# Sums for the last two batches of a fused attention and ELU-MLP kernel: taken off GpSimd, spread over three places

## The chip, the cores and the metric

The kernel runs on one core of a Trainium2 chip. The metric is the device time of one execution in microseconds (us). TensorE multiplies, VectorE (DVE in the rows) and ScalarE (ACT) work on tiles, GpSimd (POOL) can do the same as VectorE but reads no PSUM, and SyncE (SP) issues the transfers.

## The reference

Attention over 8 batches, 12 heads, 448 positions and 64 features, then an MLP over all 3584 tokens:

```python
q_n, k_n = rmsnorm(q, g_q), rmsnorm(k, g_k)
scores = q_n @ k_n.T / sqrt(64)
attn = exp(scores - max); attn = attn / (sum + 1e-9)
x = (attn @ v)                    # reshaped to (3584, 768)
h = x @ w_in                      # 768 -> 2048
g = where(h > 0, h, exp(min(h, 0)) - 1)
out = g @ w_out                   # 2048 -> 768
```

All inputs and outputs are float32.

## The kernel before

Every float32 operand of a large matmul is held as two float16 tiles, a high half and a low half (`whi`/`wli` for W_in, `who`/`wlo` for W_out, the two planes of a `gts` tile for g), and each product is three matmuls: high times high, high times low, low times high. One batch is 448 columns wide, so a matmul has a 128x128 weight tile and 448 moving columns.

The work is software-pipelined by hand. A table `SCHED` gives a half-step number to each small operation of a tile, and at each half step the kernel issues what is due and a few matmuls of the MLP of an earlier batch. Within one engine the instructions run in the order in which they were issued. Attention (scores, softmax, transposes by DMA, product with v) of a batch overlaps the MLP of the batch before it, with TensorE as the common resource.

The last two batches, 6 and 7, share their second layer (`mlp_two`). W_out is cut into quarters, and g of both batches into halves; seven block products replace eight (Strassen's scheme in Winograd's form). This needs sums of W_out's quarters (`t1` to `t4`, for each of three row groups d = 0, 1, 2) and sums of the g tiles of both batches (named `t1`, `t2` and `c22` in `sums`, beside the ones that overwrite `gts`).

- The sums of W_out's quarters are made in pieces while attention still runs (`piece_sums`, `SCHED["sums"]`). VectorE adds high and low halves, GpSimd scales and adds, ScalarE and GpSimd split the result into halves again, and SyncE stores them to DRAM (`kept`).
- During the first layer of batch 7 (`first_layer` with `m1_last`) they are loaded into the rooms of W_in that have been used up (`t_load`).
- In that same first layer each of the 16 results goes through ScalarE (exp), VectorE (the ELU), and then all the sums of g: GpSimd adds the halves of batch 6's g (`full`), forms more sums and some low halves; ScalarE forms high halves; VectorE forms the rest. `last1` and `last2` list at which half step behind the matmul each of these is issued.
- Then come 15 products of 24 matmuls each, TensorE alone; VectorE combines their banks into output tiles (`more`, line 907), and SyncE stores them (`store`).

TensorE's line 1015 is the first layer of batches 6 and 7; line 1027 is `product`. A PSUM bank is used by product after product, and a product waits until VectorE has read the bank's former content.

Of the kernel before, what the change touches and what calls it, by code (L numbers as in the profile page):

```python
# [33 lines left out]
def tile_attention_then_elu_mlp(ctx: ExitStack, tc: tile.TileContext, qk, v, v_scan, gg, w_in, w_out, out):  # L34
# [100 lines left out]
    staging = rooms[NE + 1].bitcast(F16)[:, :512].rearrange("p (i n) -> p i n", i=2)  # L135
# [665 lines left out]
    def joint_scales():  # L801
# [14 lines left out]
    kept = [  # L816
        {q: dram.tile([128, 2, KF * 128], F16, name=f"{q}{d}") for q in ("t1", "t2", "t3", "t4")}
        for d in range(3)
    ]
    tail = raws[:, 5 * S : 5 * S + 768].bitcast(F32)  # L820

    def piece_sums(d, k):

        A, Y, Z = (tail[:, a : a + 256] for a in range(0, 768, 256))

        def full(o, row, kh):
            rows = slice(kh * KF + 2 * k, kh * KF + 2 * k + 2)
            h, l = (t[d + 3 * row][:, rows].rearrange("p f n -> p (f n)") for t in (who, wlo))
            nc.vector.tensor_tensor(out=o, in0=h, in1=l, op=ALU.add)
# [9 lines left out]
        def split(o, q):  # L839
            return [  # L840
                lambda: nc.scalar.activation(staging[:, 0], o, AF.Copy),
                lambda: tt(staging[:, 1], o, staging[:, 0], ALU.subtract),
                lambda: nc.sync.dma_start(
                    out=kept[d][q][:, :, 256 * k : 256 * k + 256], in_=staging
                ),
            ]
# [18 lines left out]
        (0, "t3"), (0, "t4"), (1, "t3"), (1, "t4"), (0, "t1"), (0, "t2"),  # L865
        (1, "t1"), (1, "t2"), (2, "t3"), (2, "t4"), (2, "t1"), (2, "t2"),
    ]
    part = {dq: units[i] for i, dq in enumerate(T_ORDER)}
    h_now, t_left = [0], []

    def t_load(d, q):
        for i in (0, 1):
            nc.sync.dma_start(
                out=part[d, q][i].rearrange("p c n -> p (c n)"), in_=kept[d][q][:, i]
            )
# [52 lines left out]
    sums, temps, spots = {}, [], []  # L928

    def spaces():  # L930
        def flat(n, tag, shape, dt, k, bufs):
            t = pool.tile(shape, dt, tag=tag, name=n, bufs=bufs)
            names = " ".join(f"d{i}" for i in range(len(shape) - 1))
            t = t.rearrange(f"p {names} -> p ({names})")
            if dt == F16:
                t = t.bitcast(F32)
            return [t[:, i * S : i * S + S] for i in range(k)]

        nat_shape = [128, 2, NJ, D]
        qkt_shape = [128, 3, NJ, 128]  # L940
        spots.extend(rooms)
        spots.extend(ptall[:, i * S : i * S + S] for i in range(7))
        spots.extend(flat("sq", "qkt", qkt_shape, F16, 3, 2))
        t = [as_f32(places.pop(0)) for _ in range(3)]
        t += flat("rn", "nat", nat_shape, F32, 2, 2) + flat("rm", "nat", nat_shape, F32, 2, 2)
        t += flat("rt", "t16", [128, 2, NJ, 2, D], F16, 2, 1)
        t += flat("rq", "qkt", qkt_shape, F16, 3, 2)
        temps.append(t[:6])
        temps.append(t[6:])

    def m1_last(k, f, ph):
        sc, ui2 = (t[:, a : a + 1] for t, a in ((mscale[B - 1][0], f), (mscale[B - 1][1], 0)))
        if not spots:
            spaces()
        c = f % KF
        low = f < KF
        g = gts[f]
        e1, e2, r1, r2, r3, r4 = temps[c % 2]
        e = e1 if low else e2
        three = [as_f16(spots[i]) for i in range(3 * c, 3 * c + 3)]  # L960
        sums.update(zip([("t1", c), ("t2", c), ("c22", c)], three))
# [9 lines left out]
        def third():  # L971
            nc.vector.scalar_tensor_tensor(
                out=e, in0=ph[:, :S], scalar=sc, in1=e, op0=ALU.mult, op1=ALU.max
            )

        def full(o):
            nc.gpsimd.tensor_tensor(out=o, in0=g[:, 0], in1=g[:, 1], op=ALU.add)

        def stt(o, x, s1, y, op):
            nc.vector.scalar_tensor_tensor(out=o, in0=x, scalar=s1, in1=y, op0=ALU.mult, op1=op)  # L980

        def high(o, x, s1=1.0):
            nc.scalar.activation(o[:, 0], x, AF.Copy, scale=s1)

        def low_of(eng, o, x):
            eng.tensor_tensor(out=o[:, 1], in0=x, in1=o[:, 0], op=ALU.subtract)
# [7 lines left out]
        o1, o2, o3 = three  # L994
        return "last2", 0, [
            one, two, third, lambda: full(r4),
            lambda: high(g, e, ui2),
            lambda: nc.gpsimd.tensor_tensor(out=r3, in0=e1, in1=e2, op=ALU.add),
            lambda: stt(g[:, 1], e, ui2, g[:, 0], ALU.subtract),
            lambda: high(o1, r3, ui2), lambda: stt(r1, r3, ui2, r1, ALU.subtract),  # L1000
            lambda: high(o2, r1),
            lambda: nc.gpsimd.tensor_tensor(out=r4, in0=r4, in1=r1, op=ALU.subtract),
            lambda: stt(o1[:, 1], r3, ui2, o1[:, 0], ALU.subtract),
            lambda: high(o3, r4), lambda: low_of(nc.vector, o2, r1),
            lambda: low_of(nc.gpsimd, o3, r4),
        ]

    def first_layer(b, order, result):
        for k, f in enumerate(order):
# [11 lines left out]
            while t_left and t_left[0][0] <= k:  # L1021
                t_load(*t_left.pop(0)[1])
# [10 lines left out]
    def mlp_two():  # L1033
# [9 lines left out]
        t_left.extend((-(-4 * (i + 1) // 3) - 1, dq) for i, dq in enumerate(T_ORDER))  # L1043
# [3 lines left out]
        for h in range(h_now[0] + 1, h_now[0] + 12):  # L1047
            now, tasks[h] = tasks.get(h, []), []
            for fn, args in now:
                fn(*args)  # L1050
        banks = sb[:4] + [av] + mb
# [11 lines left out]
        for d, q in (  # L1063
            (0, "t3"), (0, "t4"), (1, "t3"), (1, "t4"), (0, "t1"), (0, "t2"), (0, "c22"),
            (1, "t1"), (1, "t2"), (1, "c22"), (2, "t3"), (2, "t4"), (2, "t1"), (2, "t2"),
            (2, "c22"),
        ):
            bank = made[d, q] = banks[n % 8]
            n += 1
            for _ in product(bank, lambda c: w_of(d, q, c), lambda c: b_of(q, c)):  # L1070
                yield None
            ub, uj = uas[d][1:]
            if q == "t2":
                u2, u3, u4 = (as_f32(places.pop(0)) for _ in range(3)) if d < 2 else ys[0]
                ys[d] = u2, u3, u4
                more(u2, bank, c11[d], uj)
                more(u4, made[d, "t1"], u2, uj)
                more(u3, made[d, "t3"], u2, uj)
                for k, row in (("t4", d), ("t1", d + 3)):
                    y = pool.tile([128, S], F32, tag="e", name="y", bufs=3)  # L1080
                    more(y, made[d, k], u3, uj)
                    store(y, row, B - 1)
# [115 lines left out]

    a, n = SCHED["sums"]
# [496 lines left out]
```

## Time and profile before

| | us |
|---|---|
| median of 3 runs (1229.64 to 1232.92) | 1229.67 |
| the profiled execution's own time | 1229.63 |
| its span, first to last instruction | 1227.8 |
| TensorE busy | 1168.1 |
| VectorE busy | 1024.3 |
| ScalarE busy | 815.0 |
| GpSimd busy | 729.0 |

Busy times are sums over the whole span. The stages differ: attention and MLP overlap until about 1088 us, the first layer of batch 7 has TensorE from there to about 1149 us, and the 15 products stand from there to the end.

### The profile page before, as it was taken

To read this page: it belongs to the slowest core of one execution; us is meant where nothing else is said; L and a number is where in the kernel's file an instruction comes from. 1 tells how busy PE (TensorE), PEld (TensorE's weight loads), DVE (VectorE), ACT (ScalarE), POOL (GpSimd) and SP (SyncE) were. 2 spreads that over 40 slices of the span, in tenths; PEclk is the share of its full clock that TensorE was granted. 3 is DMA by queue.
4 is the path that set the end of the run, shared out by engine and by line. 5 is a ranking of instruction groups with operands and counts; after the bars stand their busy time and mean duration, and the time that the engine had idled before them with its cause. 6 is when DMAs were issued, how large, how long until landed. Compare 5 with 4: busy or idle time off the path is not lost. (4 is left out here: it accounts for less than half of the span.)

```text
span 1227.8 us, 22061 instructions
## 1 busy us (share of the span) xinstructions
PE 1168.1 (95%) x7108; PEld 608.5 (50%) x7108; DVE 1024.3 (83%) x2122; ACT 815.0 (66%) x1792; POOL 729.0 (59%) x985
## 2 busy tenths in 40 slices
PE   3789999999999999999999999999999999998898
PEld 2556555555555554554444554445445545554454
DVE  7999998989986699879997899878998789649812
ACT  6999999757775577657675677666775677624400
POOL 5887668645453366756666666766566663328800
PEclk9999999999999999999999999999999999999999
DMA  7886788877777877897669876897769976533101
GB/s 252 254 240 185 188 177 200 192 162 170 141 161 176 170 149 148 176 209 158 133 154 208 185 153 130 185 205 155 142 152 190 192 146 129 103 86 103 52 23 45
DMA packets 422260, 195.85 MB, mean 160 GB/s; under 512 B 370048, under 2 KB 401536, under 8 KB 422144
## 3 DMA queue, kind: packets, MB, share of 16 engines
q1 hardware_dynamic: 422144, 194.45, 70.8%
q8 instruction: 56, 0.92, 0.3%
q14 instruction: 60, 0.49, 0.1%
HBM read 74.65 MB, written 17.30 MB: 75 GB/s over the span
## 5 line engine op out<-in xcount | busy, mean ns | idle before, releaser
L630 POOL TENSOR_SCALAR st<-st 128x1 f32<-128x1 f32 x294 | 82.7, 281 | 263.6 <-ACT w32s L626 217.9
L626 ACT ACTIVATE w32s<-s,st 128x448 f32<-128x448 f32 x242 | 152.1, 629 | 121.9 <-DVE st L610 103.9
L610 DVE TENSOR_REDUCE st<-s 128x1 f32<-128x448 f32 x336 | 203.5, 613 | 30.9 <-PE s L603 22.2
L1116 PE MATMUL m<-gall,whos 128*128 128x448 f16 x768 | 209.7, 353 | 0.0
L676 DVE SCALAR_TENSOR_TENSOR raws<-w32s,st,raws 128x448 f16<-128x448 f32 x199 | 179.5, 903 | 29.3 <-ACT raws L670 28.3
L1103 PEld LDWEIGHTS <-whis 128*128 128x128 f16 x1152 | 111.2, 98 | 110.8 <-issue 11.4
L1116 PEld LDWEIGHTS <-whos 128*128 128x128 f16 x1152 | 111.0, 98 | 107.9 <-issue 8.3
L1103 PE MATMUL m<-x,whis 128*128 128x448 f16 x578 | 157.6, 353 | 2.4 <-DVE e L759 2.4
L670 ACT ACTIVATE raws<-w32s,st 128x448 f16<-128x448 f32 x199 | 130.7, 660 | 22.0 <-DVE st L638 5.1
L1116 PE MATMUL m<-gall,wlos 128*128 128x448 f16 x384 | 135.4, 353 | 0.0
L603 PE MATMUL s<-qkt 128*64 128x448 f16 (+1 forms) x496 | 108.9, 363 | 12.4 <-DMA qkt<-t 4.9
L408 POOL TENSOR_TENSOR nat<-nat,r 128x896 f32<-128x896 f32 (+1 forms) x48 | 88.5, 1844 | 31.1 <-DVE r L398 23.9
L1116 PE MATMUL s<-gall,whos 128*128 128x448 f16 x384 | 105.3, 353 | 0.4 <-DVE gall L770 0.4
L1103 PE MATMUL m<-x,wlis 128*128 128x448 f16 x289 | 101.9, 353 | 0.0
L703 PE MATMUL av<-ptall,vt 128*64 128x448 f16 x924 | 96.2, 353 | 1.4 <-issue 1.2
L764 ACT ACTIVATE gall<-e,ui 128x448 f16<-128x448 f32 x96 | 63.5, 663 | 36.9 <-DVE e L759 36.6
L1103 PEld LDWEIGHTS <-wlis 128*128 128x128 f16 x576 | 56.3, 98 | 54.2 <-issue 3.3
L1116 PEld LDWEIGHTS <-wlos 128*128 128x128 f16 x576 | 56.3, 98 | 54.1 <-issue 3.2
L770 DVE SCALAR_TENSOR_TENSOR gall<-e,ui,gall 128x448 f16<-128x448 f32 x96 | 78.5, 819 | 1.2 <-ACT gall L764 1.2
L1103 PE MATMUL s<-x,whis 128*128 128x448 f16 x286 | 77.8, 352 | 0.3 <-DVE e L759 0.2
L703 PEld LDWEIGHTS <-vt 128*64 128x64 f16 x924 | 54.0, 110 | 37.3 <-issue 5.6
L1116 PE MATMUL s<-gall,wlos 128*128 128x448 f16 x192 | 67.7, 353 | 0.0
(330 smaller groups left out, 2758.7 us busy)
## 6 DMA issues: line engine op xcount, KB each, us to landing
nat<-in_qk SPq DMA_DIRECT2D x48, 448.0 KB, 4.5
raws<-in_w_out SPq DMA_DIRECT2D x24, 512.0 KB, 4.3
qkt<-qkt SPq DMA_DIRECT2D x96, 112.0 KB, 4.0
out<-y SPq DMA_DIRECT2D x48, 224.0 KB, 2.4
vn<-in_v SPq DMA_DIRECT2D x38, 256.0 KB, 2.9
vscan<-in_v_scan SPq DMA_DIRECT2D x36, 224.0 KB, 3.2
whos<-in_w_in SPq DMA_DIRECT2D x10, 768.0 KB, 7.5
t<-wts SPq DMA_DIRECT2D x48, 128.0 KB, 2.3
```

Of the source, the lines that this page charges most:

```text
L408: nc.gpsimd.tensor_tensor(out=n[:, a:], in0=n[:, a:], in1=r[:, a:], op=ALU.mult)
L603: nc.tensor.matmul(ps[r0 : r0 + n, :S], lhs, qq[:, 1, h * S : h * S + S], start=(t == 0), stop=(t == 2),)
L610: nc.vector.tensor_reduce(out=st[:, 0:1], in_=pss[T][:, :S], axis=AX.X, op=ALU.max, negate=True)
L626: nc.scalar.activation(e, ps, AF.Exp, bias=st[:, 0:1], accum_out=st[:, 1:2])
L630: (nc.vector if by_pe(T) else nc.gpsimd).tensor_scalar(out=st[:, 1:2], in0=st[:, 1:2], scalar1=1e-9, scalar2=2.0 ** (UP - 7) if by_pe(T) e ...
L670: nc.scalar.activation(p16[:, :S], e, AF.Copy, scale=stats[T][:, 2:3])
L676: nc.vector.scalar_tensor_tensor(out=p16[:, S:], in0=e, scalar=r, in1=p16[:, :S], op0=ALU.mult, op1=ALU.subtract)
L703: nc.tensor.matmul(av[64 * h : 64 * h + 64, :S], vs[:, h], ps[h], start=(k == 0), stop=(k == len(terms) - 1),)
L764: nc.scalar.activation(g[:, 0], e, AF.Copy, scale=1.0 if b == 0 else ui)
L770: nc.vector.scalar_tensor_tensor(out=g[:, 1], in0=e, scalar=ui, in1=g[:, 0], op0=ALU.mult, op1=ALU.subtract)
L1103: nc.tensor.matmul(ph[:, :S], w[:, c, :], x[:, r, :], start=(c == 0 and i == 0), stop=last)
L1116: nc.tensor.matmul(py[:, :S], w, g[:, r, :], start=(f == 0 and i == 0), stop=last)
```

## The change

W_out's sums: a piece is now 32 columns of all eight row blocks, so that its scale is one column of `rho`; VectorE does the additions and two fused multiply-adds, ScalarE the two remaining multiplications, GpSimd nothing. The sums are stored to DRAM in float32 and not split; splitting into halves follows after the load (`t_half`: a load, a ScalarE copy, a VectorE subtraction, in three staging tiles). Each of the 24 loads brings half of one quarter's sum: 12 are issued during batch 7's first layer, 12 behind it, in groups of three.

Sums of g: the additions of batch 6's halves (`full`, 16 of them) move to VectorE and ahead of batch 7's first layer. In the layer itself only the ELU, the two sums that overwrite `gts` and r3 stay. The sums `t2`, `t1` and `c22` are formed after the layer (`late_sums`). GpSimd has nothing to do in this tail.

The products change order: `t3` and `t4` of all three d come first, then `t2`, `t1`, `c22` for each d; banks are given by a list.

```diff
-    staging = rooms[NE + 1].bitcast(F16)[:, :512].rearrange("p (i n) -> p i n", i=2)
...
         def tt(o, x, y, op):
-            nc.gpsimd.tensor_tensor(out=o, in0=x, in1=y, op=op)
+            nc.vector.tensor_tensor(out=o, in0=x, in1=y, op=op)
+
+        def stt(o, x, i, y, op):
+            nc.vector.scalar_tensor_tensor(
+                out=o, in0=x, scalar=rho(i), in1=y, op0=ALU.mult, op1=op
+            )
 
         def mul(o, i):
-            o = o.rearrange("p (f r n) -> p f r n", f=2, r=4)
-            r = scales[f"rho{i}"][:, 4 * d : 4 * d + 4]
-            tt(o, o, r.unsqueeze(1).unsqueeze(3).broadcast_to([128, 2, 4, 32]), ALU.mult)
...
+            nc.scalar.activation(o, o, AF.Copy, scale=rho(i))
...
-            lambda: mul(A, 1), lambda: tt(Z, Z, Y, ALU.subtract), lambda: mul(Y, 2),
-            lambda: tt(Y, Y, A, ALU.subtract), lambda: mul(Z, 2),
-            *split(Y, "t1"),
-            lambda: tt(A, Z, A, ALU.add), lambda: full(Y, 0, 1),
-            *split(Z, "t3"),
-            lambda: mul(Y, 1), lambda: tt(Y, Y, A, ALU.subtract),
-            *split(A, "t2"), lambda: None, lambda: None,
-            *split(Y, "t4"),
+            lambda: mul(A, 1), lambda: tt(Z, Z, Y, ALU.subtract),
+            lambda: stt(Y, Y, 2, A, ALU.subtract), lambda: mul(Z, 2), fourth,
+            lambda: tt(A, Z, A, ALU.add),
+            lambda: nc.sync.dma_start(
+                out=kept[d][:, r], in_=tail.rearrange("p (q w) -> p q w", q=3)
+            ),
+            lambda: stt(W, W, 1, A, ALU.subtract),
+            lambda: nc.sync.dma_start(out=kept4[d][:, r, 0], in_=W),
...
+        def load():
+            nc.sync.dma_start(out=f.rearrange("p (r w) -> p r w", r=2), in_=src)
+
+        def high():
+            nc.scalar.activation(hi, v, AF.Copy)
+
+        def low():
+            nc.vector.tensor_tensor(out=lo, in0=v, in1=hi, op=ALU.subtract)
...
         if low:
             return "last1", 0, [
-                one, two, third, lambda: full(r1),
-                lambda: stt(r2, e, scales["nui2"], r1, ALU.add),
-                lambda: high(g, r2), lambda: low_of(nc.gpsimd, g, r2),
+                one, two, three, lambda: stt(r2, e, scales["nui2"], r1[c], ALU.add),
+                lambda: high(g, r2), lambda: tt(g[:, 1], r2, g[:, 0], ALU.subtract),
             ]
...
+    def late_sums(q):
...
+            if q == "t2":
+                stt(r1[c], r3[c], ui2, r1[c], ALU.subtract)
+            if q == "c22":
+                tt(r4[c], r4[c], r1[c], ALU.subtract)
...
+        t_some(3)
+        late_sums("t2")
+        t_all()
+        t_some(3)
+        late_sums("t1")
+        t_all()
+        t_some(3)
+        late_sums("c22")
+        t_all()
+        t_some(3)
+        t_all()
...
-            (0, "t3"), (0, "t4"), (1, "t3"), (1, "t4"), (0, "t1"), (0, "t2"), (0, "c22"),
-            (1, "t1"), (1, "t2"), (1, "c22"), (2, "t3"), (2, "t4"), (2, "t1"), (2, "t2"),
-            (2, "c22"),
+            (0, "t3"), (0, "t4"), (1, "t3"), (1, "t4"), (2, "t3"), (2, "t4"),
+            *((d, q) for d in range(3) for q in ("t2", "t1", "c22")),
...
-            bank = made[d, q] = banks[n % 8]
+            bank = made[d, q] = banks[(0, 1, 2, 3, 4, 5, 6, 7, 0, 1, 6, 7, 0, 2, 3)[n]]
...
-    "sums": [272, 1.18],
+    "sums": [272, 2.7],
+    "full": [666, 672],
+    "stage": 3,
-    "last1": [[1, 2, 3, 2, 4, 5, 6]],
-    "last2": [[1, 2, 3, 2, 4, 4, 5, 5, 6, 7, 7, 7, 8, 8, 9]],
+    "last1": [[1, 2, 3, 4, 5, 6]],
+    "last2": [[1, 2, 3, 4, 4, 5]],
```

What VectorE has in its queue for one pair of first-layer results of batch 7, before: `rm` and `rt` hold the pair's ELU, `raws` and `ptall` receive sums of the pair ahead of it, `m`, `s` are the banks.

```order
L967 TENSOR_SCALAR rm<-rm 128x448
L980 SCALAR_TENSOR_TENSOR gall<-x_98,ui,gall 128x448
L972 SCALAR_TENSOR_TENSOR rm<-s_71,sc,rm 128x448
L980 SCALAR_TENSOR_TENSOR ptall<-rn,ui,ptall 128x448
L980 SCALAR_TENSOR_TENSOR rq<-rm,joint,rt 128x448
L980 SCALAR_TENSOR_TENSOR raws<-rn,ui,raws 128x448
L967 TENSOR_SCALAR rt<-rt 128x448
L986 TENSOR_TENSOR raws<-ptall,raws 128x448
L972 SCALAR_TENSOR_TENSOR rt<-m_73,sc,rt 128x448
```

The same place on VectorE in the changed kernel (its own line numbers), where `rb` holds the pair's ELU and line 891 is the low half of a loaded piece:

```order
L1010 TENSOR_SCALAR rb<-rb 128x448
L990 SCALAR_TENSOR_TENSOR gall<-ra,ui,gall 128x448
L990 SCALAR_TENSOR_TENSOR rb<-s_71,sc,rb 128x448
L891 TENSOR_TENSOR wlis<-sb,whis 128x2x8x32
L990 SCALAR_TENSOR_TENSOR rb<-rb,joint,wts 128x448
L1010 TENSOR_SCALAR rb<-rb 128x448
L993 TENSOR_TENSOR gall<-rb,gall 128x448
L990 SCALAR_TENSOR_TENSOR rb<-m_73,sc,rb 128x448
L891 TENSOR_TENSOR wlis<-sc,whis 128x2x8x32
L993 TENSOR_TENSOR w32s<-rb 128x448
```

The three sums into `ptall` and `raws` have left the layer; the low half of g, r3 and three loaded pieces for every two pairs have come to VectorE.

The end of VectorE's late work in the changed kernel, with the first products' banks behind it (line 932 is `more`; `s_67` is the bank of d = 0's `t3` and, six products later, of its `c22`):

```order
L891 TENSOR_TENSOR wlis<-sa,whis 128x2x8x32
L891 TENSOR_TENSOR wlis<-sb,whis 128x2x8x32
L891 TENSOR_TENSOR wlis<-sc,whis 128x2x8x32
L891 TENSOR_TENSOR wlis<-sa,whis 128x2x8x32
L891 TENSOR_TENSOR wlis<-sb,whis 128x2x8x32
L891 TENSOR_TENSOR wlis<-sc,whis 128x2x8x32
L932 SCALAR_TENSOR_TENSOR x_91<-m_74,joint,xe 128x448
L932 SCALAR_TENSOR_TENSOR x_92<-s_67,joint,x_91 128x448
L932 SCALAR_TENSOR_TENSOR y<-s_68,joint,x_92 128x448
L932 SCALAR_TENSOR_TENSOR x_93<-s_71,joint,x_91 128x448
```

Before, the banks were read with no other VectorE work ahead of them; now all late sums and the last six loaded pieces stand in front of the first read.

## Rows read from the trace of the kernel before

**Rows 1.** The page's head and busy times over the whole span.
```profile
span 1227.8 us, 22061 instructions
PE 1168.1 (95%) x7108; PEld 608.5 (50%) x7108; DVE 1024.3 (83%) x2122; ACT 815.0 (66%) x1792; POOL 729.0 (59%) x985
```

**Rows 2.** Busy time by stage: stretch, length, engines (instructions), granted clock, DMA share, GB/s.
```profile
430.00:1020.00 590.00, 579.51 (x3393) 289.95 (x3393) 523.12 (x1045) 407.93 (x921) 387.48 (x563) 1.00 0.81 167
...
1070.00:1088.00 18.00, 18.00 (x107) 9.19 (x106) 4.62 (x8) 4.10 (x8) 2.72 (x5) 1.00 0.41 78
...
1088.00:1165.00 77.00, 67.68 (x338) 33.81 (x337) 66.74 (x73) 33.22 (x56) 59.82 (x46) 0.96 0.26 86
...
1134.00:1138.20 4.20, 3.99 (x13) 1.71 (x13) 3.70 (x7) 2.70 (x5) 3.41 (x3) 0.59 0.16 58
...
1158.60:1161.70 3.10, 3.08 (x9) 1.30 (x9) 2.30 (x4) 1.31 (x2) 2.43 (x2) 0.50 0.03 5
...
1170.00:1200.00 30.00, 30.00 (x161) 15.51 (x159) 6.72 (x11) 0.00 (x0) 0.00 (x0) 1.00 0.06 23
```

**Rows 3.** TensorE's timeline from 1088 us: start, length, instruction [idle before, releaser].
```profile
1088.17 0.54 PE L1015 MATMUL m<-x,whis 128*128 128x448 f16 x2
...
1112.00 0.54 PE L1015 MATMUL s<-x,whis 128*128 128x448 f16 x2
...
1123.39 0.54 PE L1015 MATMUL s<-x,whis 128*128 128x448 f16 x2 [1.01 <-DVE rt L972]
...
1128.50 0.54 PE L1015 MATMUL m<-x,whis 128*128 128x448 f16 x2 [1.55 <-DVE x L972]
...
1134.21 0.55 PE L1015 MATMUL m<-x,whis 128*128 128x448 f16 x2 [2.14 <-DVE x L972]
...
1149.51 0.54 PE L1027 MATMUL s<-gall,whis 128*128 128x448 f16 x2
...
1155.72 0.35 PE L1027 MATMUL s<-gall,whis 128*128 128x448 f16 x1 [2.08 <-ACT gall L983]
1158.62 0.53 PE L1027 MATMUL s<-gall,whis 128*128 128x448 f16 x1 [2.54 <-POOL gall L986]
```

**Rows 4.** VectorE's timeline from 1110 us.
```profile
1110.69 1.55 DVE L980 SCALAR_TENSOR_TENSOR w32s<-rq,ui,w32s 128x448 f16<-128x448 f32 x1
...
1113.31 1.45 DVE L986 TENSOR_TENSOR w32s<-rt,w32s 128x448 f16<-128x448 f32 x1
...
1123.26 0.61 DVE L986 TENSOR_TENSOR wts<-ptall,wts 128x448 f16<-128x448 f32 x1
...
1161.43 0.68 DVE L980 SCALAR_TENSOR_TENSOR rt<-rq,ui,rt 128x448 f32<-128x448 f32 x1
1162.03 0.68 DVE L980 SCALAR_TENSOR_TENSOR sq<-rq,ui,sq 128x448 f16<-128x448 f32 x1
...
1224.36 0.68 DVE L907 SCALAR_TENSOR_TENSOR y<-m,joint,x 128x448 f32<-128x448 f32 x1 [1.23 <-PE m L1027]
```

**Rows 5.** The same stretch, the instructions of line 832 alone (GpSimd's part of W_out's sums).
```profile
430.00:1020.00 590.00, 113.95 (x144) 1.00 0.81 167
```

**Rows 6.** Lines 829, 338 and 841: duration in ns (min/median/max), first and last start.
```profile
L829 DVE TENSOR_TENSOR raws<-whos,wlos x48: 400/414/1043, 433.6 to 997.2; 128x256 f32<-128x256 f16 x48
...
L338 DVE SCALAR_TENSOR_TENSOR wlos<-w32s,ws,whos x24: 727/743/2201, 120.7 to 261.2; 128x512 f16<-128x512 f32 x24
...
L841 ACT ACTIVATE wts<-raws x48: 398/404/417, 449.2 to 1017.6; 128x256 f16<-128x256 f32 x48
```

**Rows 7.** TensorE's waits from 300 to 1088 us: sum, times, longest.
```profile
PE s L587 <- ACT w32s L626: 5.9, 9, 1.7
PE m L1103 <- DVE e L759: 2.4, 3, 1.2
```

**Rows 8.** ScalarE's timeline at 1120 us, one high half.
```profile
1120.16 0.58 ACT L983 ACTIVATE gall<-rq 128x448 f16<-128x448 f32 x1 [0.80 <-DVE rq L980]
```

**Rows 9.** The 24 loads of 256 KB from `kept` after 1088 us, issue to landing.
```profile
DMA to landing us min/median/max: 2.5/2.9/3.9
```

More of the change, by code (lines that the diff above doesn't have):

```diff
@@ L864, in tile_attention_then_elu_mlp, with t_half, t_due @@
     T_ORDER = [
-        (0, "t3"), (0, "t4"), (1, "t3"), (1, "t4"), (0, "t1"), (0, "t2"),
-        (1, "t1"), (1, "t2"), (2, "t3"), (2, "t4"), (2, "t1"), (2, "t2"),
+        (0, "t3"), (0, "t4"), (1, "t3"), (1, "t4"), (2, "t3"), (2, "t4"),
+        (0, "t2"), (0, "t1"), (1, "t2"), (1, "t1"), (2, "t2"), (2, "t1"),
     ]
     part = {dq: units[i] for i, dq in enumerate(T_ORDER)}
[L869 to L875, printed above, removed]
+    h_now, t_left, t_slot, stage = [0], [], [0, 0], []
+    def t_half(d, q, k):
+        f = stage[t_slot[1] % 3]
+        t_slot[1] += 1
+        i = TS.index(q)
+        rows = slice(2 * k, 2 * k + 2)
+        src = kept[d][:, rows, i] if i < 3 else kept4[d][:, rows, 0]
+        hi, lo = (
+            t.rearrange("p c (r n) -> p r c n", r=4)[:, rows] for t in part[d, q]
+        )
+        v = f.rearrange("p (r c n) -> p r c n", r=2, c=KF)
+        def load():
[4 more added lines that the diff above has]
+            nc.vector.tensor_tensor(out=lo, in0=v, in1=hi, op=ALU.subtract)
+        return load, high, low
+    def t_due(k):
+        while t_left and t_left[0][0] <= k:
+            _, d, q, half = t_left.pop(0)
+            h = t_slot[0] = max(t_slot[0] + SCHED["stage"], h_now[0] + 1)
+            for x, fn in zip((0, 4, 5), t_half(d, q, half)):
+                at(int(h) + x, fn)
     uas = []
@@ L926, in mid @@
         return "mid1", 0, [lambda: y.append(second()), lambda: store(y[0], d, B - 2)]
[L928 to L943, printed above, removed]
-        t = [as_f32(places.pop(0)) for _ in range(3)]
[L945 to L949, printed above, removed]
+    sums, temps, spare, r1, r3, r4 = {}, [], [], {}, {}, {}
@@ new lines, in more_spaces, with full @@
+    def more_spaces():
+        spare.extend(ptall[:, i * S : i * S + S] for i in range(7))
+        spare.extend(rooms[: NE + 1] + rooms[NE + 2 : -1])
+        for n in ("ra", "rb"):
+            temps.append(flat(n, "qkt", [128, 3, NJ, 128], F16, 2))
+        for n in ("sa", "sb"):
+            stage.extend(flat(n, "vt", [128, NJ + 4, 2, D], F16, 2, 512))
+        stage.extend(flat("sc", "vn", [128, 4, 2, D], F32, 1, 512))
+    def full(i):
+        c, up = divmod(i, 2)
+        if i == 0:
+            first_spaces()
+        if i == 11:
+            more_spaces()
+        o = (r4 if up else r1)[c] = spare.pop(0)
+        g = gts[c + KF * up]
+        nc.vector.tensor_tensor(out=o, in0=g[:, 0], in1=g[:, 1], op=ALU.add)
@@ L957, in m1_last @@
         g = gts[f]
-        e1, e2, r1, r2, r3, r4 = temps[c % 2]
+        e1, e2, r2 = temps[c % 2]
         e = e1 if low else e2
-        three = [as_f16(spots[i]) for i in range(3 * c, 3 * c + 3)]
-        sums.update(zip([("t1", c), ("t2", c), ("c22", c)], three))
         def one():
@@ L993, in m1_last @@
             ]
-        o1, o2, o3 = three
         return "last2", 0, [
-            one, two, third, lambda: full(r4),
-            lambda: high(g, e, ui2),
-            lambda: nc.gpsimd.tensor_tensor(out=r3, in0=e1, in1=e2, op=ALU.add),
+            one, two, three, lambda: high(g, e, ui2), sum_of,
             lambda: stt(g[:, 1], e, ui2, g[:, 0], ALU.subtract),
[L1000 to L1005, printed above, removed]
-        ]
+        ]
@@ new lines, in late_sums, with make, halves_of, low @@
+    def late_sums(q):
+        ui2 = mscale[B - 1][1]
+        of = {"t1": r3, "t2": r1, "c22": r4}[q]
+        s1 = ui2 if q == "t1" else 1.0
+        def make(c):
+            if q == "t2":
+                stt(r1[c], r3[c], ui2, r1[c], ALU.subtract)
+            if q == "c22":
+                tt(r4[c], r4[c], r1[c], ALU.subtract)
+        def halves_of(c):
+            o = sums[q, c] = as_f16(spare.pop(0))
+            high(o, of[c], s1)
+            return o
+        def low(c, o):
+            if q == "t1":
+                stt(o[:, 1], of[c], ui2, o[:, 0], ALU.subtract)
+            else:
+                tt(o[:, 1], of[c], o[:, 0], ALU.subtract)
+            if q == "t1" or q == "c22":
+                spare.append(of[c])
+            if q == "c22":
+                spare.append(r1[c])
+        was = None
+        for c in range(KF):
+            make(c)
+            o = halves_of(c)
+            if was:
+                low(*was)
+            was = c, o
+        low(*was)
@@ L1050, in mlp_two, with t_some, t_all @@
                 fn(*args)
+        assert not t_left
+        late = iter([t_half(*dq, k) for dq in T_ORDER[6:] for k in (0, 1)])
+        steps = []
+        def t_some(n):
+            for load, hi, lo in [next(late) for _ in range(n)]:
+                steps.append((hi, lo))
+                load()
+        def t_all():
+            for hi, _ in steps:
+                hi()
+            for _, lo in steps:
+                lo()
+            steps.clear()
+        spare.extend(temps[0] + temps[1])
+        t_some(3)
[9 more added lines that the diff above has]
+        t_all()
         banks = sb[:4] + [av] + mb
@@ L1073, in mlp_two @@
             if q == "t2":
[L1074 to L1075 removed]
+                ys[d] = ys[0] if d == 2 else [as_f32(places.pop(0)) for _ in range(3)]
+                u2, u3, _ = ys[d]
                 more(u2, bank, c11[d], uj)
[L1077 removed]
                 more(u3, made[d, "t3"], u2, uj)
[L1079 to L1082, printed above, removed]
+                y = pool.tile([128, S], F32, tag="e", name="y", bufs=3)
+                more(y, made[d, "t4"], u3, uj)
+                store(y, d, B - 1)
+            if q == "t1":
+                u2, u3, u4 = ys[d]
+                more(u4, bank, u2, uj)
+                y = pool.tile([128, S], F32, tag="e", name="y", bufs=3)
+                more(y, bank, u3, uj)
+                store(y, d + 3, B - 1)
             if q == "c22":
@@ L1197, in mlps @@
         yield from mlp_two()
+    for i in range(2 * KF):
+        at(SCHED["full"][i > 10] + i, full, i)
     a, n = SCHED["sums"]
```

79 lines of the change are left out of this document (44 added, 35 removed).

## The prediction

> **What bounds the kernel now.** The page's busy times [rows 1] come first: TensorE 1168.1 of 1227.8 us. What can be gained is idle or slow time of TensorE, so the question is where that lies. The view by stage [rows 2] answers for two stretches: from 430 to 1020 us TensorE is busy 579.5 of 590 us, and VectorE 523.1; from 1088 to 1165 us TensorE is busy 67.7 of 77 us, VectorE 66.7, GpSimd 59.8. From 1170 on TensorE is full. TensorE's own timeline [rows 3] then gives the tail. Batch 7's first layer starts at 1088.17; seven results later it is 1112.00, so a matmul takes 23.83/126 = 0.1891 us when nothing holds it. The 288 matmuls of the layer and the 360 of the products would take 648 x 0.1891 = 122.5 us. They take until 1224.3 (VectorE reads the last bank at 1224.36 [rows 4]), which is 136.1 us. The 13.6 us between are five waits, 1.01 + 1.55 + 2.14 in the layer, which ends at 1149.5 and not at 1142.6, and 2.08 + 2.54 in the second product [rows 3]; two stretches at the lower clock behind them, 4.2 us at 0.59 and 3.1 us at 0.50 of full speed, thus 1.7 + 1.6 us lost [rows 2]; and 1 us in small pieces. The waits are for the ELU on VectorE and for low halves of g on ScalarE and GpSimd. The reader should see why VectorE is late: beside GpSimd the same instructions take 1.55 and 1.45 us that take 0.68 and 0.61 us at other moments [rows 4]. So the tail is bound by VectorE and GpSimd together from about 1105 to 1160 us, and by TensorE after that.
>
> **First layer of batch 7.** VectorE's pitch, start to start, is 0.60 us for the fused instruction (1161.43 to 1162.03), and with the same overlap of 0.08 us 0.53 for an addition of 0.61 [rows 4]. The 512-wide low half of a loaded piece is not in the trace. The nearest row is line 338, a fused 128x512 with the same kind of strided float16 output: 0.74 us against 0.68 for 448 columns, so 0.06 us more [rows 6]; I take 0.60 us pitch for the addition, with 1.0 us as the upper bound (half of the longest instruction of that line) and 0.53 as the lower. For the ELU's clamp I take 0.31, half the addition's length, as an estimate. A pair of results now costs VectorE 2 x 0.31 + 4 x 0.60 + 2 x 0.53 + 1.5 x 0.60 = 5.0 us, with no GpSimd beside it. TensorE needs 36 x 0.1891 = 6.8 us for a pair. VectorE keeps up, the three waits and the slow clock go, and the layer ends at 1088.17 + 54.5 = 1142.6: 6.9 us earlier. At 1.0 us per piece it would still be 5.6 us.
>
> **The 16 additions moved ahead.** They cost about 16 x 0.53 = 8.5 us of VectorE before 1092 us. Behind attention's last tiles there is room: from 1070 to 1088 VectorE is busy 4.6 of 18 us while TensorE is full [rows 2]. Cost 0. Without that cover a late attention tile would hold the first matmuls of the layer, at most by the few additions ahead of it (2 us).
>
> **Products.** Six products (27.2 us) that need only `gts` and W_out's sums stand first, and the second one's low halves are done about 4.2 us after the layer, before their turn. Both waits of rows 3 there and their slow clock go. But VectorE's late work now stands in front of the first reading of banks. Counted from the layer's end: 4.2 us for the last ELU and its halves; `t2` 8 x (0.60 + 0.53) and about 0.7 for the first high half on ScalarE (0.58 [rows 8]), 9.7; three pieces 1.8; `t1` 4.8; three pieces 1.8; `c22` 16 x 0.53 and a hand-over, 9.0. That is 31.3. The last three loads wait for the staging tiles that the three pieces before them free, the first 0.6 us later; a load lands after 2.9 us, between 2.5 and 3.9 [rows 9]; ScalarE's copy takes 0.6; so VectorE starts on these pieces at 35.5, ends at 37.3, and reads `s_67` (second of the fused reads, 1.2) by 38.5, with some 0.1 us for each of several hand-overs about 39.2. TensorE comes to the product that reuses `s_67` after eight products, 8 x 24 x 0.1891 = 36.3. **It waits about 3 us there.** Bounds: 0.5 us (loads at 2.5 us, no hand-overs), 8 us (pieces at 1.0 us: 12 x 0.40 = 4.8 more). Later banks are free in time, since VectorE then only has reads of 0.60 us against products of 4.5.
>
> The slow clock behind that wait: the two drops of rows 2 followed the waits of 2.14 and 2.54 us, the longest; none followed 1.01 or 1.55. So I take the 1.6 us of the second drop, with 0 as the other bound, since both drops had another wait shortly before. The Trainium skill (TensorE: Matmul & The Clock Gate, section "HAM oscillation — how this bites in real kernels") says that a pause between bursts of matmuls lets the engine fall back to half its clock, so that the next burst begins slow; by it the drop comes, as I chose, and no row here has a long wait standing alone.
>
> **W_out's sums (430 to 1020 us).** GpSimd loses 144 instructions, 114 of its 387 us [rows 5, 2]. VectorE gains 48, 24 additions and 24 fused ones of 256 columns: 0.41 [rows 6] and about 0.47, 21 us. ScalarE goes from 48 to 24 of 0.40 us [rows 6]. VectorE has 67 us idle in this stage [rows 2], and less GpSimd beside it gives something back: line 829 has a median of 414 and a longest of 1043 ns [rows 6]. TensorE's waits here are for ScalarE behind VectorE and for the ELU, 5.9 and 2.4 us [rows 7]. I take 0 in sum, between -5 (more than half of those waits go) and +5 (they grow by as much).
>
> The Trainium skill (SBUF — State Buffer, section "Who interferes with whom") says that a VectorE instruction with two inputs in SBUF and a GpSimd instruction that reads SBUF lock each other out for a whole instruction. By it every new VectorE addition here can also be held by the GpSimd work that stays, which speaks against the change; the median in rows 6 says that it seldom is.
>
> **Sum.** Lost now 13.6; lost then 3.0 + 1.6 = 4.6. Gain 9.0 us. Behind the last matmul nothing changes (one read, one store). Against the execution's own 1229.6, the median's to 0.1 us, that makes **1220.6 us**.
>
> **Rivals.**
> 1. No wait at `s_67`, or none that drops the clock: loads land at once or VectorE's late work is shorter. For it: only 3 us are missing. Against: three loads that can't start earlier. 13.6 us gained, 1216; with some waits of the middle gone, 1213.
> 2. VectorE is the bound behind the layer: pieces at 1.0 us with their strided output, wait 8 us, 1225.6. For it: no row shows such a piece. Against: line 338's median [rows 6].
> 3. The middle decides, and the kernel is slower: the 48 new instructions each held by GpSimd as line 829's longest was, 48 x 0.63 = 30 us on a VectorE with 67 idle, part of it ahead of an ELU that TensorE waits for. It outweighs the tail's gain once it adds 9.0 us to TensorE's waits, and counts as slower once it adds 12.7. With 14 us, 1235. Against: line 829 itself was seldom held [rows 6].
> 4. The change does not do what it says: the layer's waits stay because loads, staged copies and ELU hold each other in ScalarE's and VectorE's order. Then the tail keeps about its present 13.6 us, 1229. Against: 1.8 us of slack per pair.
>
> **How the numbers follow.** The forecast 0.50 (own range 1217.5 to 1224), no wait 0.18, VectorE behind the layer 0.15, the middle 0.10, no effect 0.07. A measurement of this kernel tells about 0.3%, 3.7 us, from no change: faster is below 1226.0, slower above 1233.4. Faster: 0.50 + 0.18 + most of 0.15 = 0.81. Slower: most of the 0.10, 0.08. Same 0.11. The range reaches from the first rival with a little of the middle, 1213.5, to the second with 2 us of the middle, 1227.5.
>
> **What would show it.** The first layer's TensorE rows without gaps, 54.5 us long; no two-input VectorE instruction over 0.7 us after 1092 us; the products dense but for one gap, ahead of the first product with `who` weights, released by VectorE's `more`; low clock there and nowhere else; the waits of rows 7 about as now. Wrong would make it: gaps inside the layer, released by the staged loads; pieces far over 0.7 us; or TensorE's waits between 430 and 1088 us grown by several us.

## The result, and the profile after

The changed kernel takes 1214.95 us (median of 4 runs, 1213.46 to 1217.13) against 1229.66 beside it (4 runs, 1228.78 to 1232.92): a ratio of 0.9877, 95% interval 0.9854 to 0.99. That is 14.7 us faster where 9.0 were forecast. The profiled execution took 1213.46 us.

The page's head of the changed kernel:

```profile
span 1211.7 us, 21884 instructions
PE 1162.6 (96%) x7108; PEld 605.4 (50%) x7108; DVE 1032.9 (85%) x2242; ACT 821.3 (68%) x1792; POOL 550.3 (45%) x793
```

Against [rows 1] GpSimd lost 179 us and VectorE gained 9, though it has 120 instructions more. The view by stage (columns as in [rows 2]), the stretch from 430 to 1020 us and the first layer of batch 7:

```profile
430.00:1020.00 590.00, 584.89 (x3426) 291.95 (x3425) 520.48 (x1097) 405.53 (x905) 271.92 (x422) 1.00 0.79 167
1082.10:1136.60 54.50, 54.50 (x290) 28.20 (x289) 42.81 (x76) 22.58 (x40) 0.00 (x0) 1.00 0.21 68
```

In the first of these stretches TensorE is busy 5.4 us more than in [rows 2], which the forecast did not count on. VectorE has 52 instructions more there and is busy 2.6 us less. In the first layer TensorE is full, VectorE is busy 42.8 of 54.5 us, and GpSimd does nothing. TensorE's timeline: the first layer's start, the start of the products (line 1082 is `product` here), and the only wait that is left of the tail.

```profile
1082.10 0.54 PE L1071 MATMUL m<-x,whis 128*128 128x448 f16 x2
...
1136.58 0.54 PE L1082 MATMUL s<-gall,whis 128*128 128x448 f16 x2
...
1172.71 0.35 PE L1082 MATMUL s<-w32s,wlis 128*128 128x448 f16 x1
1176.21 0.55 PE L1082 MATMUL s<-w32s,whos 128*128 128x448 f16 x2 [3.15 <-DVE x L932]
```

The layer takes 54.48 us (61.34 in [rows 3]). The three waits inside it and the two of the second product are gone. One of 3.15 us has come, ahead of the first product with `whos` weights. VectorE's timeline shows what it waits for (line 891 is the low half of a loaded piece, 932 is `more`), and the last read of a bank:

```profile
1169.24 0.69 DVE L891 TENSOR_TENSOR wlis<-sc,whis 128x512 f16<-128x512 f32 x1
1172.24 0.69 DVE L891 TENSOR_TENSOR wlis<-sa,whis 128x512 f16<-128x512 f32 x1 [2.32 <-ACT whis L888]
1172.98 0.69 DVE L891 TENSOR_TENSOR wlis<-sb,whis 128x512 f16<-128x512 f32 x1
1174.15 0.69 DVE L891 TENSOR_TENSOR wlis<-sc,whis 128x512 f16<-128x512 f32 x1 [0.48 <-ACT whis L888]
1174.76 0.68 DVE L932 SCALAR_TENSOR_TENSOR x<-m,joint,xe 128x448 f32<-128x448 f32 x1
1175.47 0.68 DVE L932 SCALAR_TENSOR_TENSOR x<-s,joint,x 128x448 f32<-128x448 f32 x1
...
1208.21 0.68 DVE L932 SCALAR_TENSOR_TENSOR y<-s,joint,x 128x448 f32<-128x448 f32 x1 [3.27 <-PE s L1082]
```

VectorE stands still for 2.32 us in front of the last three pieces; their loads start only when the three before them have freed the staging tiles (the first at 1168.75 us, landing 2.8 us later). The read of the `s` bank that starts at 1175.47 is what TensorE waits for. TensorE's waits from 300 to 1088 us:

```profile
PE av L702 <- DMA ptall<-raws: 2.4, 4, 0.9
PE s L586 <- ACT w32s L625: 2.1, 6, 0.6
PE m L1190 <- DVE e L758: 0.3, 1, 0.3
PE m L1071 <- DVE e L758: 0.2, 1, 0.2
```

The two kinds of [rows 7] fell from 8.3 to 2.4 us (5.9 to 2.1 and 2.4 to 0.3); a wait of 2.4 us for a transfer has come.

**Where the time came from.** To compare stages of executions that do not start alike, three marks on TensorE are used: the first score burst (line 586, 587 before) after 443 us, the last score burst, and the first layer's start. In the changed kernel the bursts are these:

```profile
443.41 0.73 PE L586 MATMUL s<-qkt 128*128 128x448 f16 x3
...
1046.06 0.54 PE L586 MATMUL s<-qkt 128*128 128x448 f16 x2
```

The middle (first to second mark) is 602.65 us here and 1052.12 - 444.36 = 607.76 before. The tail (third mark to the span's end) is 1211.7 - 1082.10 = 129.6 and 1227.8 - 1088.17 = 139.6. The span is 16.1 us shorter: 5.1 from the middle, 10.0 from the tail, 6.9 of them in the layer, and about 1.0 from a start that differs between executions. The stretch from 430 to 1020 us holds more work in a faster kernel; between the first two marks the work is the same. There VectorE's busy time fell from 538.4 to 531.7 us with 49 instructions more, first before, then changed:

```profile
444.36:1052.12 607.76, 597.27 (x3489) 298.70 (x3488) 538.41 (x1083) 420.23 (x948) 389.46 (x571) 1.00 0.80 165
```
```profile
443.41:1046.06 602.65, 597.22 (x3490) 298.42 (x3489) 531.72 (x1132) 414.90 (x925) 275.72 (x429) 1.00 0.79 166
```

### The profile page after: what moved, and what is told of

The parts are those of the page before. It is cut to its first block, busy times and chain, and to the rows that moved or that the text cites. A ratio compares the mean times of both kernels' runs of the same rounds, so it can differ in the third digit from the quotient of the medians.

```text
span 1211.7 us, 21884 instructions
## 1 busy us (share of the span) xinstructions
PE 1162.6 (96%) x7108; PEld 605.4 (50%) x7108; DVE 1032.9 (85%) x2242; ACT 821.3 (68%) x1792; POOL 550.3 (45%) x793
## 5 line engine op out<-in xcount | busy, mean ns | idle before, releaser
L629 POOL TENSOR_SCALAR st<-st 128x1 f32<-128x1 f32 x294 | 80.1, 272 | 382.1 <-ACT w32s L625 341.2
L675 DVE SCALAR_TENSOR_TENSOR raws<-w32s,st,raws 128x448 f16<-128x448 f32 x199 | 174.1, 876 | 23.6 <-ACT raws L669 23.4
L769 DVE SCALAR_TENSOR_TENSOR gall<-e,ui,gall 128x448 f16<-128x448 f32 x96 | 70.3, 733 | 1.3 <-ACT gall L763 1.3
```

The lines of the kernel that those rows point to most:

```text
L629: (nc.vector if by_pe(T) else nc.gpsimd).tensor_scalar(out=st[:, 1:2], in0=st[:, 1:2], scalar1=1e-9, scalar2=2.0 ** (UP - 7) if by_pe(T) e ...
L675: nc.vector.scalar_tensor_tensor(out=p16[:, S:], in0=e, scalar=r, in1=p16[:, :S], op0=ALU.mult, op1=ALU.subtract)
L769: nc.vector.scalar_tensor_tensor(out=g[:, 1], in0=e, scalar=ui, in1=g[:, 0], op0=ALU.mult, op1=ALU.subtract)
```

## The experiments

Unless a base is named, each kernel is the changed one with the edit shown. Each ratio is to the kernel before as it was measured beside that run (1229.66 us in the first two rows, 1231.58 for e1 to e4, 1231.01 for e5 to e8, 1231.99 for e9 to e11). Middle and tail are those of the one profiled execution of each, by the marks above:

| | median us | ratio to before | middle | tail |
|---|---|---|---|---|
| before | 1229.66 | 1 | 607.8 | 139.6 |
| changed | 1214.95 | 0.9877 | 602.7 | 129.6 |
| e1, GpSimd reads in the middle | 1228.76 | 0.9989 (0.9973 to 1.0005) | 615.9 | 129.5 |
| e2, GpSimd writes in the middle | 1221.26 | 0.9909 (0.988 to 0.9937) | 606.8 | 131.1 |
| e3, before without GpSimd's sums | 1221.08 | 0.9916 (0.9896 to 0.9936) | 597.6 | 140.9 |
| e4, without VectorE's new sums | 1209.45 | 0.9822 (0.9802 to 0.9842) | 594.4 | 131.7 |
| e5, banks read first | 1211.64 | 0.9852 (0.9839 to 0.9866) | 602.5 | 126.2 |
| e6, GpSimd reads in the layer | 1234.1 | 1.0028 (1.0015 to 1.0041) | 602.5 | 147.7 |
| e7, additions back in the layer | 1215.26 | 0.9884 (0.987 to 0.9899) | 602.2 | 131.3 |
| e8, changed again | 1219.72 | 0.9906 (0.989 to 0.9922) | 602.5 | 129.4 |
| e9, one-input sums | 1212.48 | 0.9839 (0.9818 to 0.9859) | 597.6 | 132.4 |
| e10, changed, third time | 1214.56 | 0.9865 (0.9842 to 0.9888) | 602.0 | 131.3 |
| e11, banks read first, again | 1211.95 | 0.9835 (0.982 to 0.985) | 603.0 | 126.2 |
| e12, changed, one execution | 1216.83 | | 602.4 | 131.2 |

The eight executions with the changed kernel's middle (changed, e5 to e8, e10 to e12) lie within 602.0 to 603.0, so a middle that differs by 2 us is taken as a real difference.

**Middle: what GpSimd's work costs (e1, e2, e3).** Theory: GpSimd's reading instructions hold VectorE's two-input ones; their removal pays, the rest follows. Rival: only the queues matter.

```diff
+ ball = rooms[NE + 1].bitcast(F16)[:, 512:768].rearrange("p (a n) -> p a n", a=2)
+ def ballast():                            # e1
+     i2 = ident.unsqueeze(1).broadcast_to([128, 2, 128])
+     nc.gpsimd.tensor_tensor(out=ball, in0=i2, in1=i2, op=ALU.add)
+ for i in range(144):
+     at(272 + int(i * 2.56), ballast)
...
+ ball = rooms[NE + 1].bitcast(F16)[:, 512:896]
+ def ballast():                            # e2
+     for _ in range(2):
+         nc.gpsimd.memset(ball, 0.0)
...
- nc.gpsimd.tensor_tensor(out=o, in0=x, in1=y, op=op)
+ pass                                      # e3, of before
```

> The changed kernel with 144 GpSimd additions of 256 columns put back between 430 and 1020 us; they read a constant, write a scratch tile, and nobody waits for them. Theory lock: TensorE's waits of the middle shrank by 5 us because GpSimd's reading instructions no longer hold VectorE's two-input ones; then these waits come back, the first layer of batch 7 starts near 1087 instead of 1082 us, the time is about 1220 us, ratio 0.992, and VectorE's mean for the low halves of the probabilities (876 ns now) rises to 900 or more. Theory queue: the gain came from GpSimd's small softmax instructions no longer standing behind long ones; then the same 1220, but VectorE's durations stay. Rival: the middle gained by the new places of VectorE's instructions; then 1215, ratio 0.988.

> As the run with 144 additions, but each is two GpSimd memsets, which fill GpSimd's queue and read nothing from SBUF. Theory lock: VectorE's two-input instructions are not held by it, time stays near 1215 us, ratio 0.988. Theory queue: the softmax instructions stand behind them all the same, 1218 to 1220 us, ratio 0.991.

> The kernel before without the 144 GpSimd instructions of W_out's sums (the stored sums are then not the right ones; VectorE's additions, ScalarE's copies and all transfers stay, nothing is moved to VectorE). Theories lock and queue: the first layer of batch 7 starts 5 us earlier, near 1083 us, or more than that since VectorE has no new work; the tail keeps its waits; about 1224 us, ratio 0.995. Rival, new places of VectorE's instructions: 1229, ratio 1.0.

The middle, mark to mark, for e1, then e2, then e3, and e1's waits of TensorE from 300 us to the layer:

```profile
443.77:1059.64 615.87, 599.24 (x3489) 299.95 (x3488) 555.90 (x1132) 415.68 (x926) 381.19 (x571) 1.00 0.77 163
```
```profile
445.50:1052.32 606.82, 597.81 (x3490) 298.10 (x3489) 537.08 (x1132) 415.64 (x926) 389.39 (x712) 1.00 0.78 165
```
```profile
445.05:1042.63 597.58, 595.03 (x3490) 297.80 (x3489) 513.62 (x1082) 419.84 (x949) 272.23 (x429) 1.00 0.80 168
```
```profile
PE s L586 <- ACT w32s L625: 6.8, 9, 1.8
PE av L702 <- DMA ptall<-raws: 4.7, 5, 1.5
PE m L1190 <- DVE e L758: 2.5, 3, 1.3
PE m L1203 <- DVE gall L769: 1.9, 2, 1.4
```

Some 105 us of reading GpSimd work lengthen the middle by 13.2 us and bring back the waits of [rows 7]; VectorE is busy 24.2 us longer with the same 1132 instructions. As much GpSimd time that only writes (113.7 against 105.5 us) costs 4.2 us, and VectorE's busy time grows by 5.4. Taking the 144 instructions out of before shortens its middle by 10.2 us and takes 24.8 us from VectorE's busy time, though VectorE's own instructions are the same.

Single instructions of e2 (430 to 1020 us) show whom the memsets hold. Of VectorE's instructions with two SBUF inputs, 43 ran beside memsets alone and took at most 1.05 times the shortest of their line; 254 ran beside other GpSimd work, all of which reads SBUF, and took up to 3.4 times that. So about two thirds of the cost of such work hang on its reading beside VectorE; the rest is its place in GpSimd's queue or something else that was not taken apart.

The expectations were off in size: e1 took 1228.8 us where 1220 were expected, and e3's middle gained 10.2 us where 5 were. The sign named for e1, line 675's mean (the low halves of the probabilities), hardly moved (876 to 882 ns over the whole span); other two-input lines carry the rise, the low halves of g from 733 to 846 ns.

**Middle: what VectorE's new work costs (e4, e9).** The 24 additions and 24 fused ones are left out (e4), or read one tile where they read two (e9).

```diff
- nc.vector.tensor_tensor(out=o, in0=x, in1=y, op=op)
- nc.vector.scalar_tensor_tensor(out=o, in0=x, scalar=rho(i), in1=y, op0=ALU.mult, op1=op)
+ pass                                                              # e4, both
...
+ nc.vector.tensor_scalar(out=o, in0=y, scalar1=1.0, scalar2=None, op0=ALU.mult)     # e9
+ nc.vector.tensor_scalar(out=o, in0=y, scalar1=rho(i), scalar2=None, op0=ALU.mult)
```

> The changed kernel without the 48 new VectorE instructions of W_out's sums (the stored sums are then not the right ones; the additions of halves, ScalarE's multiplications and the transfers stay). If VectorE's 21 us of new work in the middle cost TensorE something, the first layer of batch 7 starts earlier than at 1082 us, by up to 3 us, 1212 us; if they are hidden, as the prediction had it, 1215 us, ratio 0.988.

> The changed kernel, with the 48 new VectorE instructions of W_out's sums (24 additions, 24 fused) put as tensor-scalar instructions of the same 256 columns that read one tile where they read two (the values of part of W_out's sums are thus left out). It asks why they cost some 8 us of the middle. Theory A, they cost because a two-input instruction and a reading GpSimd instruction hold each other: one-input instructions give most of the 8 us back, 1207 to 1211 us, the other sums' lines in the middle as short as without the 48. Theory B, they cost because they stand in VectorE's queue ahead of attention's work: as many instructions remain, 1213 to 1216 us, the middle 6 us or more slower than without the 48.

The middle, mark to mark, for e4, then e9:

```profile
444.53:1038.94 594.41, 594.00 (x3489) 297.77 (x3488) 508.68 (x1084) 415.06 (x925) 275.48 (x429) 1.00 0.80 169
```
```profile
447.55:1045.11 597.56, 595.23 (x3490) 297.89 (x3489) 522.59 (x1132) 415.26 (x925) 277.27 (x429) 1.00 0.80 168
```

Without the 48 instructions the middle is 8.2 us shorter, where up to 3 were expected, and TensorE has hardly a gap; they did cost. VectorE is busy 23.0 us less. With one input 5.1 of the 8.2 us come back. But this does not tell the theories apart, as two views of single lines show, the changed kernel's additions first, then e9's instructions in their place (ns: shortest/median/longest):

```profile
L835 DVE TENSOR_TENSOR raws<-raws x23: 400/414/1378, 449.5 to 1016.5; 128x256 f32<-128x256 f32 x23
```
```profile
L835 DVE TENSOR_SCALAR raws<-raws x23: 268/280/1243, 453.6 to 1016.3; 128x256 f32<-128x256 f32 x23
```

The one-input form is a third shorter by its median, and its longest is still four times that: it takes less of the queue and can be held too. In the middle the 48 instructions take 25.0 us in the changed kernel and 19.3 in e9, and what they take above the medians of their lines is 3.7 us against 4.4: they are held no less with one input. So theory A's premise, that one input takes the hold away, fails. Theory B's sign, a middle 6 us or more above e4's, did not come either: it is 3.1. The gain of 5.1 us goes with 5.7 us less of VectorE's own time in these instructions, which speaks for the queue; but other lines are held a little less too (the low halves of g take 706 ns on average, 731 in the changed kernel), and how VectorE's 8.2 us divide into hold and queue stays open. The time says as little: 1212.48 lies between the two expectations.

**The layer: is it GpSimd's absence, and are the additions free (e6, e7)?** e6 gives GpSimd six additions per pair that nothing needs; e7 puts the 16 additions of batch 6's halves back, on VectorE.

```diff
+ def ballast():                                                    # e6
+     for _ in range(6):
+         nc.gpsimd.tensor_tensor(out=ball[0], in0=r3[c], in1=r3[c], op=ALU.add)
- one, two, three, lambda: high(g, e, ui2), sum_of,
+ one, two, three, lambda: high(g, e, ui2), sum_of, ballast,
- "last2": [[1, 2, 3, 4, 4, 5]],
+ "last2": [[1, 2, 3, 4, 4, 4, 5]],
...
- for i in range(2 * KF):                                           # e7
-     at(SCHED["full"][i > 10] + i, full, i)
+ one, two, three, lambda: full(2 * c), ...
+ one, two, three, lambda: full(2 * c + 1), ...
...
```

> The changed kernel with six GpSimd additions of 448 columns per pair of first-layer results put back in batch 7's first layer; they read r3 and write a scratch tile, and nobody waits for them. Theory lock (before, VectorE was late in the layer because GpSimd's reading instructions held its two-input ones): these take 1.4 us again and more, VectorE needs about 5.0 + 5.5 x 0.7 = 8.9 us a pair, the layer is 10 to 17 us longer and has gaps, about 1226 us. Rival (VectorE and TensorE were late because they waited for GpSimd's results, and because VectorE had the sums in the layer): GpSimd's presence alone costs nothing, 1215 us.

> The changed kernel with the 16 additions of batch 6's halves back in the first layer, but on VectorE, one per result. By the sum of the prediction VectorE then needs 5.0 + 2 x 0.53 = 6.1 us for a pair against TensorE's 6.8, so the layer stays without gaps and the time stays within 1 us of the changed kernel, ratio 0.988. Rival: VectorE's order makes it late already at this load; gaps in the layer, 3 us or more.

VectorE's timeline in e6's layer, and TensorE's waits in its tail:

```profile
1101.11 1.35 DVE L995 TENSOR_TENSOR gall<-rb,gall 128x448 f16<-128x448 f32 x1
1102.38 0.67 DVE L992 SCALAR_TENSOR_TENSOR rb<-m,sc,rb 128x448 f32<-128x448 f32 x1
...
1106.55 1.35 DVE L992 SCALAR_TENSOR_TENSOR ra<-ra,joint,rn 128x448 f32<-128x448 f32 x1
1107.82 1.12 DVE L1012 TENSOR_SCALAR ra<-ra 128x448 f32<-128x448 f32 x1
```
```profile
PE s L1088 <- DVE x L932: 6.5, 1, 6.5
PE s L1088 <- ACT gall L998: 3.0, 1, 3.0
PE m L1077 <- DVE ra L992: 3.0, 2, 1.6
PE s L1088 <- DVE gall L995: 2.7, 1, 2.7
PE m L1077 <- DVE rb L992: 0.8, 1, 0.8
```

Beside GpSimd, instructions with two inputs in SBUF can take 1.35 us, twice their time, and the clamp, which has one, 1.12 us where it takes 0.39 in the changed kernel; the one that reads PSUM (`m`) stays at 0.67. The Trainium skill (SBUF — State Buffer, "Who interferes with whom") says that VectorE and GpSimd share one pair of ports, held by one of them for a whole instruction: a VectorE instruction with two SBUF inputs contends for it with a GpSimd instruction that reads SBUF and not with one that only writes, and a form such as `tensor_scalar` contends when it runs in a fast mode that uses the pair. The rows of e6, e9 and e2 agree.

The layer takes 58.7 us against 54.5 in the changed kernel and 61.3 before, with 39.1 us of GpSimd work beside it (46.7 before); 10 to 17 us more were expected. GpSimd runs on until 1162 us, 19 us behind the layer's end, and there the waits of the second product come back (3.0 and 2.7 us) and the one at the reused bank grows to 6.5. In all the tail grows by 18 us and the whole gain is gone, with all else as in the changed kernel.

In e7 the layer has no gap with VectorE busy 46.5 of its 54.5 us (42.8 above), and its time is that of the changed kernel: the additions could have stayed.

**The lone wait and the clock (e5, e8, e10 to e12).** e5 and e11 move d = 0's first reads ahead of the last three pieces; e8, e10 and e12 are the changed kernel itself.

```diff
  t_some(3)
- t_all()
  banks = sb[:4] + [av] + mb
...
  store(y, d + 3, B - 1)
+ if d == 0:
+     t_all()
```

> The changed kernel with one thing moved: the splitting of the last three loaded pieces (needed only by d = 2's products) is issued behind VectorE's first five reads of banks instead of ahead of them. If the wait of 3.15 us ahead of d = 0's c22 comes from those pieces standing in front of the read of its bank, it goes, nothing else changes, and the time falls by 3.1 us, to ratio 0.985. Rival: the sums themselves are the late part, or the pieces come too late for d = 2; then a wait of 1 to 3 us stands there or ahead of d = 2's t2, and the time stays within 1 us.

> The changed kernel as it is, beside the others on the same chip: ratio 0.988 again.

> The changed kernel itself once more, beside the version that reads the first banks earlier. If the 3-us wait ahead of the reused bank costs its own length alone: 3 to 4 us above that version. If in some executions the clock falls behind the wait as the prediction said: executions of about 1219 among those of 1213 to 1215, and in the records of such an execution a stretch behind the wait with a granted clock near 0.5.

> The version that reads d = 0's first banks ahead of the last loaded pieces, again, on the same chip as the changed kernel: 1211 to 1214 us and no TensorE wait in the tail. If the changed kernel's spread up to 1220 us comes from its wait, this one has no execution above 1216; if it is the chip's, or the middle's, it has them too.

> One more profiled execution of the changed kernel. If it is one of the longer ones, its windows show where the time is: by the prediction's step, 1.6 us at a granted clock near 0.5 right behind the wait ahead of the reused bank; by the rival that the middle varies, the tail as in the first profile and the first layer of batch 7 starting later than 1082 us.

TensorE behind the wait in e10, and the window there:

```profile
1175.95 0.93 PE L1082 MATMUL s<-w32s,whos 128*128 128x448 f16 x2 [3.23 <-DVE x L932]
1176.67 0.58 PE L1082 MATMUL s<-w32s,wlos 128*128 128x448 f16 x1
```
```profile
1175.90:1179.10 3.20, 3.15 (x9) 1.34 (x10) 1.87 (x3) 0.00 (x0) 0.00 (x0) 0.50 0.31 120
```

Here the granted clock is 0.50, 1.2 of 2.4 GHz, behind the wait; a matmul takes 0.58 us where it takes 0.35 in the changed kernel's rows above. The tail is 131.3 us against 129.6: the drop costs 1.7. e12 shows it too (131.2). Nine profiled executions had the wait. The tail is 129.4 to 129.6 in three (changed, e8, e1; waits of 2.93 to 3.15 us) and 131.1 to 132.4 in six (e2, e4, e7, e9, e10, e12; waits of 3.05 to 3.23 us). So waits of the same length are followed by the drop in some executions and not in others; what decides was not found.

Without the wait (e5, e11) the tail is 126.2 us in both: 3.4 less than without the drop, 5 less than with it. Eight executions of this version took 1210.9 to 1214.3 us, thirteen of the changed kernel in rounds 1213.2 to 1220.0. It beats both kernels: 0.9852 and 0.9835 against 0.9906 and 0.9865 of the changed kernel beside them (e8, e10); the intervals of the first pair are apart, those of the second overlap a little.

Some results were off: e8's ratio is 0.9906 where 0.988 was expected, and e10's median is 2.6 us above e11's where 3 to 4 were. Five of the thirteen took 1217.1 to 1220.0 us, and none of the eight without the wait did, which by e11's expectation points at the wait. The drop alone does not explain them: the four over 1218 us have a mean granted clock of 0.999 on record, which leaves at most 1.8 us for slow clock in the whole execution, and e10's profiled execution took 1214.8 us with the drop. e7's profile, of an execution of 1219.1 us, shows what adds up there: its middle is 602.2 us, its first mark lies at 447.70 us, 4.3 later than in the changed kernel, and its tail is 1.7 us longer. Across the profiled executions the burst that is at 310.17 us in the changed kernel lies between 309.96 and 314.11, whatever the kernel. So a late start and the drop together make some 6 us; no execution of the changed kernel itself over 1217 us was profiled, and for those the cause stays open.

## Why the prediction was right, and where it was off

- **The layer without gaps: right.** 54.5 us forecast, 54.48 measured. The piece whose price was open took 0.69 us at a pitch of 0.60, the value chosen. No two-input VectorE instruction behind the layer's start took over 0.7 us. e6 shows that GpSimd's reads beside VectorE are enough for gaps (4.2 of the 6.9 us come back), e7 that more VectorE instructions are not.
- **The additions moved ahead, cost 0: right.** They run behind the second mark, and from there to the layer's start it is 36.0 us in before, in the changed kernel and in e7, which has none of them there. But they need not have moved.
- **The second product's waits go: right;** e6 brings them back.
- **The new wait at `s_67` of about 3 us: right**, 3.15, released by VectorE's `more`, with the late loads as the reason. Counted from the layer's end, VectorE starts the last pieces at 35.7 us (35.5 forecast) and has read `s_67` at 39.6 (39.2), and TensorE is there at 36.5 (36.3). e5 takes the wait away by order alone. The lower bound of 0.5 us does not follow from its terms, which give about 1.2.
- **The slow clock behind it, 1.6 us: right in size (1.7 in e10, 2.8 at most in e9), but not in every execution.** It came in six of nine. The Trainium skill (TensorE: Matmul & The Clock Gate, "HAM oscillation — how this bites in real kernels") ties the fall to the length of the pause, which the forecast's sentence on it leaves out; here the length does not separate the six from the three. In the profiled execution 1.6 us of the sum is therefore missing.
- **W_out's sums, "0 in sum": this step was mis-sized.** It measured -5.1 us, just past the end of its range of -5 to +5, and it was no sum of small terms: taking the work from GpSimd gave 10.2 us (e3), giving VectorE 48 instructions cost 8.2 (e4), and the remaining 3.1 us is by subtraction what else changed (fewer ScalarE copies, other stores); that remainder was not measured by itself. In VectorE's busy time the forecast had 21 us of new work, near the 23.0 of e4, but no figure for what comes back, which was 24.8 (e3). The argument was that line 829's median [rows 6] is near its shortest, so VectorE is seldom held. A median hides this: the low halves of g on VectorE have the same median before and after, 673 ns, but means of 860 and 731 ns (the view by line, 430 to 1020 us, before and after):

```profile
L770 DVE SCALAR_TENSOR_TENSOR gall<-e,ui,gall 128x448 f16<-128x448 f32 x68 | 58.5, 860 | 0.0
```
```profile
L769 DVE SCALAR_TENSOR_TENSOR gall<-e,ui,gall 128x448 f16<-128x448 f32 x70 | 51.2, 731 | 0.0
```

The step looked at one line's median where the sum over all lines was asked for. Nor did VectorE's idle 67 us cover the new work.

With the drop, 8.4 us of the tail and 5.1 of the middle make 13.5; without it, 10.0 and 5.1 make 15.1. The medians differ by 14.7, and by 11.3 and 17.4 where the changed kernel ran again (e8, e10). The measured 1214.95 lies below the forecast's own range of 1217.5 to 1224. That the wide range holds it is in part luck: it reached down to 1213.5 for the first rival's sake. The first rival's 1213 with some of the middle's waits gone was near in number, but its reason, no wait at `s_67`, did not come. The third rival had the middle's sign wrong: VectorE's additions do cost, yet GpSimd's absence gives more. Nothing was found for the other two.

## What to carry to other kernels

Work moved from GpSimd to VectorE has two prices, and both should be worked out: what VectorE spends on it, and what all of VectorE's two-input instructions get back from it. Read the mean against the minimum of such lines, not the median, take the sum over the lines, and compare stretches that hold the same work. Where late work stands in one queue with the reads that free PSUM banks, put the reads first: here that was worth as much as its wait, and sometimes a slow clock more.

## What the runs showed of the hardware

- GpSimd work that only writes added 5.4 us to VectorE's busy time in the middle (537.1 against 531.7) and 4.2 us to the stage; reading work of about the same length added 24.2 and 13.2.
- Beside GpSimd memsets alone, 43 VectorE instructions with two SBUF inputs took at most 1.05 times the shortest of their line; beside GpSimd work that reads, such instructions took up to 3.4 times (e2).
- A one-input clamp on VectorE is held beside GpSimd as well: 1.12 us against 0.39 (e6).
- Behind a wait of about 3.1 us that stands alone, the granted clock falls to 0.50 in some executions and stays at 1.00 in others, of the same kernel too: 3.23 us (e10) and 3.15 us (changed).
- TensorE's middle repeats to 1 us (602.0 to 603.0 in eight executions) while the start of the pipeline differs by 4 us between executions; comparing marks inside the span shows differences that the whole time hides.
